# q and k of the third late unit loaded into the free tile of x, and the visits of the first late segment set anew

## The chip, the core and the metric

The kernel runs on one core of one Trainium2 chip. The metric is the device time of an execution in microseconds (us). The kernel before took 726.04 us (median of 3 runs, 725.66 to 726.95). The profiled execution is one of them, the one of 725.66 us; the span from its first to its last instruction is 723.9 us.

## What is computed

Attention over chunks, then one gated feed-forward layer. q, k and v are [4, 8, 768, 64] (batch, heads, sequence, head size); every chunk of 32 queries sees 8 memory positions, 16 positions to the left, its own 32 and 8 to the right. The result is laid out as 3072 tokens of 512 values and goes through the second part.

```python
for c in range(nc):                                   # 24 chunks of 32 queries
    k_full = np.concatenate([mem_k, k[:, :, l_start:r_end]], axis=2)
    v_full = np.concatenate([mem_v, v[:, :, l_start:r_end]], axis=2)
    a = softmax(scale * np.matmul(q_c, k_full.transpose(0, 1, 3, 2)))
    out[:, :, c_start:c_end] = np.matmul(a, v_full)
...
xn = x / rms * rms_g                                  # x: 3072 x 512
g = xn @ w_gate                                       # 512 x 1536
silu = g * (1.0 / (1.0 + np.exp(-g)))
return (silu * (xn @ w_val) @ w_out)                  # w_out: 1536 x 512
```

## The kernel before

**Units, blocks, segments.** Attention is cut into 32 units: one unit is one batch, one half of its sequence (384 queries, 12 chunks) and two heads. Four units fill one block, 384 tokens by 512 values, held in a tile `x`. There are 8 blocks. The feed-forward part goes block by block: for each of 12 columns f of the hidden layer TensorE (PE) makes g (12 matmuls of 128x384, `pg`, L591) and v (12 more, `pv`, L591), and one column later the output part (9 matmuls of 128x512, `po`, L629). Each f32 matrix is split in a high and a low part, so every product takes three matmuls. Between them the other engines make the hidden value of the column: ACT `t` (tanh, L598), DVE `t` (L602, which reads `pg` and frees it; L605, which reads `pv`), ACT `hh` (its high part, a cast, L255), DVE `hl` (its low part, L614). The output part reads `hh` in its first two matmuls of three and `hl` in the third. `t`, `hh`, `hl`, `pg` and `pv` have one buffer each.

**The written-out part.** Units 0 to 15 and their feed-forward columns are in a string of tokens, `ORDER`, that sets every engine's order by hand. It covers blocks 0 and 1: columns 0 to 4 of block 0 and all 12 of block 1 (items 0 to 16 of `SEQ`; item 15 is column 10 of block 1, item 16 its column 11). Near its end stand the tokens R0 to R4 for the first late unit, unit 16 (batch 2, first half, heads 0 and 1): R0 loads its q and k, R2 transposes them, R4 loads its v. The string ends with `o14 I Ha R3 L v16 k15a l15 h16 o15 i16 j16`: the matmuls v of item 16, the cast `hh` of item 15 on ACT (k15a), its `hl` on DVE (l15), its output part on PE (o15).

**The late part.** After it come the segments: columns 5 to 11 of block 0 (the first late segment), then blocks 2 to 7. PE's order there is that of the code; a scheduler places the other engines' instructions by priority. Units 16 to 31 are made in pairs by `late_steps`, in steps that the table `VISITS` puts into gaps of a segment: gap 2(f - first f) stands behind the g of column f, the next gap behind its v. Step "v" of pair n holds the PE work: the transposes `pT` (L377) of the pair before, the scores `s` (L346) of pair n, the outputs `o` (L398) of the pair before; then DVE writes the outputs into `x` (`stage_r`). It also transposes q and k of the first unit of pair n + 1 on DVE (`stage_t`, behind the last DVE instruction placed so far). Step "t" does so for the second unit of that pair and loads the first one of pair n + 2. Step "n" scales a finished block. A block's `x` is turned (`xT`, L470) and split at the end of its segment.

**A late unit's loads.** `load_qk` issues 8 DMAs on SP's queue, 4 of q (L193) and 4 of k (L195), by turns. They fill the tiles `qn` and `kn`, one buffer each, so a unit's loads wait until DVE has transposed the unit before (L315 twice for q, L320 once for k). `load_v` first has ACT copy the memory's values into the unit's v tile (`kv<-memV`, L255), POOL adds ones (L214), and SP issues 5 DMAs of v (L228, L239). For unit 16 the tile `memV` is filled anew for batch 2 by two DMAs on SP's queue (L210) ahead of that copy. After its transposes two small copies on ACT (L328, L329) finish a unit's k. DMAs of one queue are issued in order, and an instruction that waits holds all behind it on its engine.

The late tiles of one unit of a pair share buffers with tiles of the first part: `late_buffers(0)` clears a tile (`qp`, L132) just after the written-out part.

Of the kernel before, what the change touches and what calls it, by code (L numbers as in the profile page):

```python
# [8 lines left out]
F32 = mybir.dt.float32  # L9
# [10 lines left out]
CH = 32  # L20
LC, RC = 16, 8
KC = NM + LC + CH + RC
DM, FF = 512, 1536
P = 128
NG = H // 2
HT = 384
NT = HT // P
NC = HT // CH
# [6 lines left out]
YMAX = 0x1DFE / 0x1000 * 2.0 ** -96  # L35


VISITS = (((1, "v"), (4, "t"), (5, "v"), (8, "t"), (11, "v"), (12, "n")),
# [31 lines left out]
def tile_kernel(ctx: ExitStack, tc: tile.TileContext, q, k, v, mem_k, mem_v,  # L70
# [3 lines left out]
    p1 = ctx.enter_context(tc.tile_pool(name="p1", bufs=1))  # L74
# [33 lines left out]
    def on_pe(ins):  # L108
        if pinned:
            tc.keep_in_program_order(ins)  # L110

    def psum_a(name):
        return psa.tile([P, 512], F32, name=name, tag="at")

    def psum_m(tag, name):
        return psm.tile([P, 512], F32, name=name, tag=tag)


    NE = NG * 2
# [42 lines left out]
    def pt_of(u):  # L162

        return pts[1 + u % 2] if u < NE else late["pt", 1 - u % 2]
# [9 lines left out]
    def load_qk(u):  # L174
        b, hf, g = units[u]
        h0 = 2 * g
        t0 = hf * HT
        d = st.setdefault(u, {})
        if u < NE:

            k0 = t0 - hf * CH
            for n, src, r0, rows in (("q", q, t0, HT), ("k", k, k0, HT + CH)):
                x = d[n] = early.tile([P, 8, D], F32, name=f"{n}f{u}", tag=f"{n}f{u % NG}")[0:rows // 4]
                nc.sync.dma_start(out=x.rearrange("p (h r) d -> p h (r d)", h=2),
                                  in_=src[b, h0:h0 + 2, r0:r0 + rows].rearrange("h (p r) d -> p h (r d)", r=4))
            return

        d["q"] = qn = p1.tile([P, NC, CH], F32, name=f"qn{u}", tag="qn")
        d["k"] = kn = p1.tile([P, NC + 1, CH], F32, name=f"kn{u}", tag="kn")
        k0 = t0 - hf * CH  # L190
        for w in range(4):
            hh, e = w // 2, CH * (w % 2)
            nc.sync.dma_start(out=qn[CH * w:CH * w + CH],  # L193
                              in_=q[b, h0 + hh, t0:t0 + HT, e:e + CH].rearrange("(c p) d -> p c d", p=CH))
            nc.sync.dma_start(out=kn[CH * w:CH * w + CH],  # L195
                              in_=k[b, h0 + hh, k0:k0 + HT + CH, e:e + CH].rearrange("(c p) d -> p c d", p=CH))

    def load_v(u):
        stage_v(u)
        dma_v(u)  # L200

    def stage_v(u, e="a"):
        b, hf, g = units[u]
        h0, h1 = 2 * g, 2 * g + 2
        t0 = hf * HT
        d = st.setdefault(u, {})
        d["v"] = vw = unit_tile(u, [P, NJ, 2, D + 1], "vw", NG)
        if hf == 0 and g == 0 and b > 0:
            for cp in range(2):
                nc.sync.dma_start(out=memV[64 * cp:64 * cp + NM], in_=mem_v[b].rearrange("h m d -> m h d"))  # L210

        mv = memV[:, h0:h1].unsqueeze(1).broadcast_to([P, NJ, 2, D])
        copy(e, vw[:, :, :, 0:D], mv)
        nc.gpsimd.tensor_copy(out=vw[:, :, :, D], in_=ones[hf])  # L214

    def dma_v(u, e="s"):
        b, hf, g = units[u]
        h0, h1 = 2 * g, 2 * g + 2
        t0 = hf * HT
        vw = st[u]["v"]  # L220
        W = KC - NM
        for cp in range(2):
            base = 64 * cp
            s0 = t0 + CH * cp - LC
            ja, jb = 0, NJ
            eng = nc.scalar if e == "a" else nc.sync
            if hf == 0 and cp == 0:
                eng.dma_start(out=vw[base + NM + LC:base + KC, 0, :, 0:D],  # L228
                              in_=v[b, h0:h1, 0:W - LC].rearrange("h s d -> s h d"))
                ja = 1  # L230
            if hf == 1 and cp == 1:
                r0 = s0 + 64 * (NJ - 1)
                eng.dma_start(out=vw[base + NM:base + KC - RC, NJ - 1, :, 0:D],
                              in_=v[b, h0:h1, r0:r0 + W - RC].rearrange("h s d -> s h d"))
                jb = NJ - 1
            for hh in range(2):
                vs = v[b, h0 + hh]
                src = bass.AP(vs.tensor, vs.offset + (s0 + 64 * ja) * D, [[D, W], [64 * D, jb - ja], [1, D]])
                eng.dma_start(out=vw[base + NM:base + KC, ja:jb, hh, 0:D], in_=src)  # L239
# [64 lines left out]
    def stage_t(u):  # L304

        stage_ta(u)
        new_kw(u)
        stage_tb(u)
        stage_tc(u)
# [40 lines left out]
    def stage_m(u):  # L350
        stage_ma(u)
        stage_mb(u)
# [18 lines left out]
    def stage_p(u, tag=None):  # L371
        d = st[u]
        tag = tag or (None if u >= NG else "o0")
        t = psum_m(tag, f"pT{u}") if tag else psum_a(f"pT{u}")
        pe = d["p"].rearrange("p j k -> p (j k)")
        for i in range(NT):
            on_pe(nc.tensor.transpose(out=t[:, i * P:(i + 1) * P], in_=pe[:, i * P:(i + 1) * P], identity=ident))  # L377
        d["t"] = t
# [10 lines left out]
    def stage_o(u, tag=None):  # L389
        d = st[u]  # L390
        pt = pt_of(u)
        tag = tag or (None if u >= NG else f"o{1 + u % 2}")
        o = psum_m(tag, f"o{u}") if tag else psum_a(f"o{u}")
        for i in range(NT):
            for hh in range(2):
                for par in range(2):
                    c0 = (2 * i + hh) * (D + 1)
                    on_pe(nc.tensor.matmul(o[64 * par:64 * par + 64, c0:c0 + D + 1],  # L398
                                     lhsT=pt[:, i, 2 * par + hh].rearrange("p c q -> p (c q)"),
                                     rhs=d["v"][:, 2 * i + par, hh, :], start=True, stop=True))  # L400
        d["o"] = o
# [313 lines left out]
    def new_x():  # L715
        return p1.tile([P, NT, H, D], F32, name="x", tag="x")
# [3 lines left out]
    def behind_last(u):  # L720
        done = next(i for i in reversed(nc.cur_bb.bb.instructions) if i.engine == nc.vector.engine)
        with tc.issue_after(done):
            stage_t(u)

    def late_steps():


        pairs = [(u, u + 1) for u in range(NE, len(units), 2)]
        for n in range(len(pairs) + 1):
            old = pairs[n - 1] if n else ()  # L730
            cur = pairs[n] if n < len(pairs) else ()
            new = pairs[n + 1] if n + 1 < len(pairs) else ()
            for u in old[0:1]:
                if u % NG == 0:
                    late_x["x"] = new_x()
            x = late_x.get("x")
            with tc.high_priority():
                for i, u in enumerate(old):
                    stage_p(u, None if i else "g")
                for u in old:  # L740
                    stage_c(u)
            if not cur:
                yield "p"
            with tc.high_priority():
                for u in cur:
                    stage_s(u)
                for u in cur:
                    stage_m(u)
                for u in cur:
                    stage_e(u)  # L750
                for i, u in enumerate(old):
                    stage_o(u, "v" if cur and i else None)
                for u in old:
                    stage_r(u, x)
                for u in new[0:1]:
                    behind_last(u)
            for u in new[0:1]:
                load_qk(u + 1)
            for u in cur if n else ():
                load_v(u)  # L760
            yield "v"
            if n and n % 2 == 0:
                with tc.high_priority():
                    stage_n(x)
                yield "n"
            if new:
                with tc.high_priority():
                    behind_last(new[1])
                if n + 2 < len(pairs):
                    load_qk(pairs[n + 2][0])  # L770
            yield "t"

    x = new_x()
# [28 lines left out]
    def tok_R(n):  # L802
        if n == 0:
            load_qk(NE)
        if n == 1:
            late_buffers(1)
        if n == 2:
            stage_t(NE)
        if n == 3:
            late_pt()  # L810
        if n == 4:
            load_v(NE)
            load_qk(NE + 1)

    def tok_N(n):
        sp["ss"] = stage_n0(blk["x"])
# [83 lines left out]
        late_buffers(0)  # L900
        stage_t(NE + 1)
    load_v(NE + 1)
    load_qk(NE + 2)
    pinned.append(True)

    def split_x(x, first, rest):
# [17 lines left out]
    for sg, (blk, f0) in enumerate(segments):  # L924
        po = [psm_o(i) for i in range(NT)] if sg else sp["po", 0]
        last = sg == len(segments) - 1
        steps = {} if last else dict(VISITS[min(sg, 2) + (sg == len(segments) - 2)])

# [57 lines left out]
```

## Time and profile before

| | before |
|---|---|
| median of 3 runs | 726.04 us |
| the profiled execution | 725.66 us |
| its span | 723.9 us |
| granted TensorE clock, mean | 0.995 |
| busy: PE, DVE, ACT, POOL | 708.6, 382.1, 284.2, 35.5 us |
| mean DMA rate | 69 GB/s |

Times in the profile count from the span's start. A row of the timeline gives start, duration, engine, line, operation, out<-in, shape, count, and in brackets the idle time of the engine before it with what ended it. A row of the waits gives who waited for whom, the sum, the count and the longest. A row of the stages gives start:end, its length, then each engine's busy time with its count, the granted TensorE clock (1.00 is full speed), the share of the DMA engines and GB/s.

### The profile page before, as it was taken

To read this page: it belongs to the slowest core of one execution; us is meant where nothing else is said; L and a number is where in the kernel's file an instruction comes from. 1 tells how busy PE (TensorE), PEld (TensorE's weight loads), DVE (VectorE), ACT (ScalarE), POOL (GpSimd) and SP (SyncE) were. 2 spreads that over 40 slices of the span, in tenths; PEclk is the share of its full clock that TensorE was granted. 3 is DMA by queue.
4 is the path that set the end of the run, shared out by engine and by line. 5 is a ranking of instruction groups with operands and counts; after the bars stand their busy time and mean duration, and the time that the engine had idled before them with its cause. 6 is when DMAs were issued, how large, how long until landed. Compare 5 with 4: busy or idle time off the path is not lost.

```text
span 723.9 us, 13126 instructions
## 1 busy us (share of the span) xinstructions
PE 708.6 (98%) x5136; PEld 656.0 (91%) x5136; DVE 382.1 (53%) x727; ACT 284.2 (39%) x600; POOL 35.5 (5%) x143
## 2 busy tenths in 40 slices
PE   7889999999999999999999999999999999999997
PEld 7778999998989999999999999999998999999997
DVE  3888999975663625444273534536254332432222
ACT  4899666543353315332153312433143221331112
POOL 3300000010010001000010000000010000000000
PEclk8999999999999999999999999999999999999999
DMA  8994554425532402304041120413111110010001
GB/s 173 206 255 147 175 194 127 125 46 123 97 60 75 78 9 42 77 11 84 0 77 52 34 53 1 84 44 66 18 35 28 44 39 1 1 45 0 1 1 43
DMA packets 143173, 50.20 MB, mean 69 GB/s; under 512 B 126984, under 2 KB 134536, under 8 KB 143112
## 3 DMA queue, kind: packets, MB, share of 16 engines
q1 hardware_dynamic: 139832, 44.49, 26.8%
q10 hardware_dynamic: 3280, 4.88, 1.9%
q8 instruction: 40, 0.66, 0.4%
q14 instruction: 21, 0.17, 0.1%
HBM read 43.06 MB, written 6.29 MB: 68 GB/s over the span
## 4 chain that ended last, share of the span: by engine, by line
PE 89%; ACT 4%; DVE 2%; DMA 2%; issue 1%; SPq 1%; POOL 0%; ACTq 0%; DVEq 0%; POOLq 0%
PE po L629 27%; PE pv L591 26%; PE pg L591 26%; PE s L346 3%; PE o L398 2%; PE xT L470 1%; PE pT L377 1%; ACT junk L428 1%; DMA memV<-in_mem_v_dram 1%; ACT pt L255 1%; DMA kv<-in_v_dram 1%; ACT qb L255 0%; ACT wy L539 0%; ACT ws L538 0%; SPq L195 0%
## 5 line engine op out<-in xcount | busy, mean ns | idle before, releaser
L591 PE MATMUL pg<-xh,wh_g 128*128 128x384 f32 x384 | 130.0, 339 | 0.7 <-DVE t L602 0.7
L591 PE MATMUL pv<-xh,wl_v 128*128 128x384 f32 x384 | 129.5, 337 | 0.5 <-DVE wl_v L562 0.5
L591 PE MATMUL pv<-xh,wh_v 128*128 128x384 f32 x384 | 129.7, 338 | 0.0
L591 PE MATMUL pv<-xl,wh_v 128*128 128x384 f32 x384 | 129.6, 337 | 0.0
L591 PE MATMUL pg<-xh,wl_g 128*128 128x384 f32 x384 | 129.5, 337 | 0.0
L591 PE MATMUL pg<-xl,wh_g 128*128 128x384 f32 x384 | 129.4, 337 | 0.0
L255 ACT CAST hh<-t 128x384 fp32r<-128x384 f32 x95 | 48.6, 512 | 201.9 <-PE po L629 177.8
L629 PE MATMUL po<-wh_o,hh 128*128 128x512 f32 x285 | 114.7, 402 | 0.3
L629 PE MATMUL po<-wh_o,hl 128*128 128x512 f32 x285 | 113.1, 397 | 0.0
L602 DVE SCALAR_TENSOR_TENSOR t<-t,pg 128x384 f32<-128x384 f32 x96 | 53.0, 552 | 112.8 <-ACT t L598 112.4
L629 PE MATMUL po<-wl_o,hh 128*128 128x512 f32 x285 | 112.3, 394 | 0.0
L614 DVE TENSOR_TENSOR hl<-t,hh 128x384 fp32r<-128x384 f32 x95 | 52.5, 553 | 104.7 <-ACT hh L255 99.9
L598 ACT ACTIVATE t<-pg 128x384 f32<-128x384 f32 x96 | 47.1, 491 | 122.8 <-PE pg L591 114.9
L605 DVE TENSOR_TENSOR t<-t,pv 128x384 f32<-128x384 f32 x95 | 52.5, 553 | 75.5 <-PE pv L591 74.9
L591 PEld LDWEIGHTS pg<-xh,wh_g 128*128 128x128 f32 x384 | 72.0, 188 | 4.6 <-DVE t L602 0.9
L591 PEld LDWEIGHTS pg<-xl,wh_g 128*128 128x128 f32 x384 | 72.1, 188 | 3.5
L591 PEld LDWEIGHTS pv<-xh,wl_v 128*128 128x128 f32 x384 | 72.0, 188 | 0.8 <-DVE wl_v L562 0.8
L591 PEld LDWEIGHTS pv<-xh,wh_v 128*128 128x128 f32 x384 | 72.1, 188 | 0.4
L591 PEld LDWEIGHTS pv<-xl,wh_v 128*128 128x128 f32 x384 | 72.1, 188 | 0.3
L591 PEld LDWEIGHTS pg<-xh,wl_g 128*128 128x128 f32 x384 | 72.0, 188 | 0.0
L629 PEld LDWEIGHTS po<-wh_o,hl 128*128 128x128 f32 x285 | 53.5, 188 | 14.4 <-DVE hl L614 2.0
L629 PEld LDWEIGHTS po<-wh_o,hh 128*128 128x128 f32 x285 | 53.5, 188 | 10.5 <-ACT hh L255 1.7
(124 smaller groups left out, 772.3 us busy)
## 6 DMA issues: line engine op xcount, KB each, us to landing
kn<-in_k_dram SPq DMA_DIRECT2D x96, 52.0 KB
qn<-in_q_dram SPq DMA_DIRECT2D x96, 48.0 KB
out_dram<-ob ACTq DMA_DIRECT2D x18, 256.0 KB
ws<-in_moe_w_gate_dram SPq DMA_DIRECT2D x4, 1024.0 KB
ws<-in_moe_w_val_dram SPq DMA_DIRECT2D x4, 1024.0 KB
ws<-in_moe_w_out_dram SPq DMA_DIRECT2D x4, 1024.0 KB
kv<-in_v_dram SPq DMA_DIRECT2D x48, 84.0 KB
kv<-in_v_dram SPq DMA_DIRECT2D x48, 70.0 KB
```

The costliest lines, as they stand in the source:

```text
L255: return nc.scalar.copy(out, in_)
L346: on_pe(nc.tensor.matmul(s[64 * par:64 * par + 64, o:o + KC], lhsT=qb[:, c].rearrange("p s q -> p (s q)"), rhs=kw[:, c], start=True, stop= ...
L377: on_pe(nc.tensor.transpose(out=t[:, i * P:(i + 1) * P], in_=pe[:, i * P:(i + 1) * P], identity=ident))
L398: on_pe(nc.tensor.matmul(o[64 * par:64 * par + 64, c0:c0 + D + 1], lhsT=pt[:, i, 2 * par + hh].rearrange("p c q -> p (c q)"), rhs=d["v"][: ...
L428: nc.scalar.activation(junk[:, 0:(g1 - g0) * P], x[:, i, 2 * g0:2 * g1].rearrange("p h d -> p (h d)"), AF.Square, accum_out=ss[:, i:i + 1])
L470: on_pe(nc.tensor.transpose(out=t[:, i * P:(i + 1) * P], in_=tiles[i][:, kt * P:(kt + 1) * P], identity=ident))
L591: on_pe(nc.tensor.matmul(ps[:, 0:HT], lhsT=weight(a, n, f, kt), rhs=xs[c][:, kt], start=cnt == 0, stop=cnt == 3 * NKT - 1))
L598: nc.scalar.activation(t, g, AF.Tanh, scale=0.5)
L602: nc.vector.scalar_tensor_tensor(out=t, in0=t, scalar=1.0, in1=g, op0=ALU.add, op1=ALU.mult)
L605: nc.vector.tensor_tensor(out=t, in0=t, in1=vv, op=ALU.mult)
L614: nc.vector.tensor_tensor(out=hl, in0=t, in1=hh.bitcast(F32), op=ALU.subtract)
L629: on_pe(nc.tensor.matmul(po[i], lhsT=h[a][:, i * P:(i + 1) * P], rhs=weight(c, "o", f), start=f == 0 and n == 0, stop=f == NF - 1 and n == 2))
```

## The change

- **A tile of its own for q and k of unit 18, the third late unit (L188, L189).** Until step "v" of the second pair, nothing is in the tile of `x`, since blocks 0 and 1 are done with it. Unit 18 loads q and k into one tile `qkn` with the tag "x". So its loads no longer wait for unit 17's transposes, and unit 19 takes the turn of 18 in `qn` and `kn`.
- **Loads one turn earlier (L811 to L813, L903, L757, L769).** Token R4 now loads q and k of unit 17 first, then v of 16, then q and k of 18. Behind the written-out part stand v of 17 and q and k of 19 (before: 18). Step "v" of the first pair loads nothing more.
- **The first transposes of the third pair (L753 to L756).** In the second pair's step "v", `stage_t` of unit 20 now stands ahead of `stage_r` of units 16 and 17, and not behind it.
- **Visits of the first late segment (L38).** The first "t" moves from gap 4 to 2, the third "v" from 11 to 9, and "n" from 12 to 10. The other segments keep theirs.

What is computed is the same, and so is the number of each engine's instructions but for rows of SP that are counted apart.

```diff
-VISITS = (((1, "v"), (4, "t"), (5, "v"), (8, "t"), (11, "v"), (12, "n")),
+VISITS = (((1, "v"), (2, "t"), (5, "v"), (8, "t"), (9, "v"), (10, "n")),
...
-        d["q"] = qn = p1.tile([P, NC, CH], F32, name=f"qn{u}", tag="qn")
-        d["k"] = kn = p1.tile([P, NC + 1, CH], F32, name=f"kn{u}", tag="kn")
+        if u == NE + 2:
+
+            t = p1.tile([P, NT * DM], F32, name=f"qkn{u}", tag="x")
+            d["q"] = qn = t[:, 0:NC * CH].rearrange("p (c d) -> p c d", d=CH)
+            d["k"] = kn = t[:, NC * CH:(2 * NC + 1) * CH].rearrange("p (c d) -> p c d", d=CH)
+        else:
+            d["q"] = qn = p1.tile([P, NC, CH], F32, name=f"qn{u}", tag="qn")
+            d["k"] = kn = p1.tile([P, NC + 1, CH], F32, name=f"kn{u}", tag="kn")
...
+                for u in new[0:1] if n == 1 else ():
+                    behind_last(u)
                 for u in old:
                     stage_r(u, x)
-                for u in new[0:1]:
+                for u in new[0:1] if n != 1 else ():
                     behind_last(u)
-            for u in new[0:1]:
+            for u in new[0:1] if n else ():
                 load_qk(u + 1)
...
         if n == 4:
+            load_qk(NE + 1)
             load_v(NE)
-            load_qk(NE + 1)
+            load_qk(NE + 2)
...
     load_v(NE + 1)
-    load_qk(NE + 2)
+    load_qk(NE + 3)
```

Three places of the engines' orders follow, before and now (now the code's lines stand 6 to 10 lower; the number behind a tile's name tells one buffer's use from the next).

SP's queue from the end of unit 16's q and k (`qn_1844`, `kn_1845`) on; `kv_1882` is unit 16's v tile. Before:

```order
L195 DMA kn_1845<-in_k_dram 32x13x32 [waits DMAHW4_49]
L210 DMA memV<-in_mem_v_dram 8x8x64 [waits DMAHW5_49]
L210 DMA memV<-in_mem_v_dram 8x8x64 [waits DMAHW6_49]
L228 DMA kv_1882<-in_v_dram 40x2x64 [waits DMAHW7_49,DVE_49,Pool_49]
L239 DMA kv_1882<-in_v_dram 56x5x64 [waits DMAHW0_49]
```

Now, with `qn_1910` and `kn_1911` for unit 17:

```order
L201 DMA kn_1845<-in_k_dram 32x13x32 [waits DMAHW4_49]
L199 DMA qn_1910<-in_q_dram 32x12x32 [waits DMAHW5_49,DMAHW3_49,DMAHW7_49,DMAHW1_49,DVE_49]
L201 DMA kn_1911<-in_k_dram 32x13x32 [waits DMAHW4_49,DMAHW2_49,DMAHW6_49,DMAHW0_49,DVE_49]
L199 DMA qn_1910<-in_q_dram 32x12x32
L201 DMA kn_1911<-in_k_dram 32x13x32
L199 DMA qn_1910<-in_q_dram 32x12x32
L201 DMA kn_1911<-in_k_dram 32x13x32
L199 DMA qn_1910<-in_q_dram 32x12x32
L201 DMA kn_1911<-in_k_dram 32x13x32
L216 DMA memV<-in_mem_v_dram 8x8x64 [waits DMAHW5_49]
L216 DMA memV<-in_mem_v_dram 8x8x64 [waits DMAHW6_49]
L234 DMA kv_1882<-in_v_dram 40x2x64 [waits DMAHW7_49,Pool_49]
```

The two DMAs of `memV` stood right behind unit 16's loads; now unit 17's eight stand between, and the first two of these wait for DVE.

DVE behind the written-out part, from item 16's `t` (L605) on. Before:

```order
L605 TENSOR_TENSOR t<-t,pv 128x384 [waits DVE_49,PE_49]
L132 MEMSET qp_1976 128x1536
L614 TENSOR_TENSOR hl<-t,hh 128x384 [waits PE_49,Activation_49]
L315 STREAM_TRANSPOSE qp_1976<-qn_1919 64x12x32 [waits DMAHW6_49,DMAHW4_49,DVE_49]
L602 SCALAR_TENSOR_TENSOR t<-t,pg 128x384 [waits Activation_49]
L315 STREAM_TRANSPOSE qp_1976<-qn_1919 64x12x32 [waits DMAHW2_49,DMAHW0_49]
L320 STREAM_TRANSPOSE kv_1978<-kn_1920 128x13x32 [waits DMAHW5_49,DMAHW7_49,DMAHW3_49,DMAHW1_49]
```

Now:

```order
L611 TENSOR_TENSOR t<-t,pv 128x384 [waits DVE_49,PE_49]
L132 MEMSET qp_1985 128x1536
L326 STREAM_TRANSPOSE kv_1987<-kn_1911 128x13x32 [waits DMAHW4_49,DMAHW6_49,DMAHW2_49,DMAHW0_49]
L321 STREAM_TRANSPOSE qp_1985<-qn_1910 64x12x32 [waits DMAHW7_49,DMAHW5_49,DVE_49]
L321 STREAM_TRANSPOSE qp_1985<-qn_1910 64x12x32 [waits DMAHW3_49,DMAHW1_49]
L620 TENSOR_TENSOR hl<-t,hh 128x384 [waits PE_49,Activation_49]
L608 SCALAR_TENSOR_TENSOR t<-t,pg 128x384 [waits Activation_49]
```

Unit 17's three transposes moved ahead of item 16's `hl`.

DVE in the first late segment, from the `hl` of column 6 to the reader of column 7's `pg`. Before:

```order
L614 TENSOR_TENSOR hl<-t,hh 128x384 [waits PE_49,Activation_49]
L315 STREAM_TRANSPOSE qp_1976<-qn_2095 64x12x32 [waits DMAHW5_49,DMAHW4_49]
L315 STREAM_TRANSPOSE qp_1976<-qn_2095 64x12x32 [waits DMAHW6_49,DMAHW2_49]
L320 STREAM_TRANSPOSE kv_1978<-kn_2096 128x13x32 [waits DMAHW3_49,DMAHW7_49,DMAHW1_49,DMAHW0_49]
L602 SCALAR_TENSOR_TENSOR t<-t,pg 128x384 [waits Activation_49]
```

Now, from unit 18's and 19's transposes on:

```order
L326 STREAM_TRANSPOSE kv_1882<-qkn_1929 128x13x32 [waits DMAHW7_49,DMAHW5_49,DMAHW1_49]
L321 STREAM_TRANSPOSE qp_1985<-qn_2003 64x12x32 [waits DMAHW2_49,DMAHW0_49]
L326 STREAM_TRANSPOSE kv_1987<-kn_2004 128x13x32 [waits DMAHW5_49,DMAHW7_49,DMAHW3_49,DMAHW1_49]
L608 SCALAR_TENSOR_TENSOR t<-t,pg 128x384 [waits Activation_49]
L611 TENSOR_TENSOR t<-t,pv 128x384 [waits DVE_49,PE_49]
L620 TENSOR_TENSOR hl<-t,hh 128x384 [waits PE_49,Activation_49]
L608 SCALAR_TENSOR_TENSOR t<-t,pg 128x384 [waits Activation_49]
```

Unit 19's transposes moved from between column 6's `hl` and column 7's reader (L602, now L608) to ahead of column 6's reader.

## The prediction

> **What bounds the kernel now.** I read the page first, then PE's waits, then the timeline of each engine around them.
>
> ```profile
> span 723.9 us, 13126 instructions
> PE 708.6 (98%) x5136; PEld 656.0 (91%) x5136; DVE 382.1 (53%) x727; ACT 284.2 (39%) x600; POOL 35.5 (5%) x143
> ```
>
> PE works nearly all the time. So only PE's gaps can be won, and any new gap costs its whole length. PE's waits from 100 us on, with the sum, the count and the longest:
>
> ```profile
> PE pT L377 <- DVE t L602: 1.4, 1, 1.4
> PE xT L470 <- DVE x L451: 0.4, 1, 0.4
> ...
> 220.00:700.00 480.00, 479.79 (x3310) 446.95 (x3310) 204.46 (x409) 143.88 (x330) 14.26 (x59) 1.00 0.17 37
> ```
>
> There are two, both in the first late segment; the stage row from 220 to 700 shows PE at 479.79 of 480. The change can win 1.4 + 0.4 = 1.8 us and no more. The first gap in the timeline:
>
> ```profile
> 177.22 0.49 ACT L598 ACTIVATE t<-pg 128x384 f32<-128x384 f32 x1 [1.84 <-PE pg L591]
> 177.41 0.47 SPq L195 DMA_DIRECT2D kn<-in_k_dram  x1
> 178.87 0.58 DVE L315 STREAM_TRANSPOSE qp<-qn 64x384 f32<-64x384 f32 x1 [1.25 <-DMA qn<-in_q_dram]
> 179.63 0.61 DVE L320 STREAM_TRANSPOSE kv<-kn 128x416 f32<-128x416 f32 x1 [0.18 <-DMA kn<-in_k_dram]
> 180.17 0.52 DVE L602 SCALAR_TENSOR_TENSOR t<-t,pg 128x384 f32<-128x384 f32 x1
> 180.74 0.55 PE L377 MATMUL pT<-ident,kv 128*128 128x128 f32 x3 [1.44 <-DVE t L602]
> ```
>
> Column 7's `pg` could be read from 177.71, when ACT ends, but DVE stands before unit 19's transposes until its DMAs land. PE needs that buffer for `pT`.
>
> **What is won.** Unit 18 has its own tile, so unit 19's loads wait for unit 17's transposes alone, and unit 19's own now stand ahead of column 6's reader. Then nothing of DMA is between column 7's g and its reader: the 1.4 goes. The third "v" and "n" come two gaps earlier, so `x` is scaled a whole column before `xT` needs it: the 0.4 goes too. The PE work of the moved visits is the same, since the same matmuls stand between a v and a `po` one column earlier. Sum: minus 1.8, if nothing else becomes late there (below).
>
> **What the queue of SP costs.** Two engines around the end of the written-out part, first SP and DVE, then ACT and PE:
>
> ```profile
> 145.86 0.73 SPq L210 DMA_DIRECT2D memV<-in_mem_v_dram  x2
> 153.31 1.17 DVE L315 STREAM_TRANSPOSE qb<-qn 64x384 f32<-64x384 f32 x2
> 154.52 0.61 DVE L320 STREAM_TRANSPOSE kv<-kn 128x416 f32<-128x416 f32 x1
> ...
> 155.58 0.84 ACT L255 COPY kv<-memV 128x768 f32<-128x768 f32 x1
> 156.80 0.63 ACT L255 CAST wh_o<-wy 128x512 fp32r<-128x512 f32 x1 [0.38 <-DVE wy L554]
> 157.33 0.51 ACT L255 CAST hh<-t 128x384 fp32r<-128x384 f32 x1
> 157.61 0.63 DVE L562 TENSOR_TENSOR wl_o<-wy,wh_o 128x512 fp32r<-128x512 f32 x1
> 158.15 0.55 DVE L614 TENSOR_TENSOR hl<-t,hh 128x384 fp32r<-128x384 f32 x1
> 158.34 0.40 PE L629 MATMUL po<-wh_o,hh 128*128 128x512 f32 x1
> 158.81 0.45 PE L629 MATMUL po<-wh_o,hl 128*128 128x512 f32 x1
> ```
>
> `memV` was asked for at 145.86, ten us before ACT's copy. Now its two DMAs queue behind unit 17's eight, and these wait for unit 16's transposes, the last of which ends at 154.52 + 0.61 = 155.13. How long eight take behind a transpose is seen at a later unit:
>
> ```profile
> 188.00 0.61 DVE L320 STREAM_TRANSPOSE kv<-kn 128x416 f32<-128x416 f32 x1
> 188.64 0.32 SPq L195 DMA_DIRECT2D kn<-in_k_dram  x1
> ...
> 191.56 0.47 SPq L195 DMA_DIRECT2D kn<-in_k_dram  x1
> ```
>
> The last of the eight is out at 192.03, 3.4 us behind the transpose's end. So `memV` is issued at 158.6 and, its second half, at 159.0. From issue to the reader: 1.97 to 2.22 us for q and k above (177.41 to 179.63). For `memV` itself the DMA view, in slices of 0.1 us from 145 on, bounds it from below:
>
> ```profile
> DMA  9983399721699413995333311100000000000000
> ```
>
> The last packets end at 147.6, 1.3 us behind the second issue (146.3). So ACT can copy between 160.3 and 161.2; I take 160.8, since a semaphore follows the last packet. ACT works in order, and behind the copy stand the cast of `wh_o` and item 15's `hh`. From 160.8: copy 0.84, `wh_o` 0.63, overlapped to 0.53 (156.80 to 157.33), `hh` 0.51, done at 162.7. DVE behind it: `wl_o` from 162.2, `hl` from 162.8 to 163.35. PE's third matmul of item 15 started 0.11 behind `hl` (158.70 to 158.81), so now at 163.46 instead of 158.81. PE has nothing else to do, as its order is fixed: **plus 4.65**, from 4.15 to 5.05 by the two landing times.
>
> **What the moved transposes cost.** Item 16's `hl` and the matmuls around it:
>
> ```profile
> 160.74 1.34 DVE L132 MEMSET qp<- 128x1536 f32 x1 [0.27 <-PE po L629]
> 162.00 0.49 DVE L614 TENSOR_TENSOR hl<-t,hh 128x384 fp32r<-128x384 f32 x1
> 162.61 0.39 PE L629 MATMUL po<-wh_o,hh 128*128 128x512 f32 x1
> 163.07 0.39 PE L629 MATMUL po<-wh_o,hl 128*128 128x512 f32 x1
> ```
>
> Unit 17's three transposes now come between the memset and `hl`: 1.17 + 0.61 = 1.78. Their data are there by then (issued until 158.6). `hl` ended at 162.49, on this clock now at 164.27, and the third matmul follows at 164.38 instead of 163.07: **plus 1.3**. Both chains hang on item 15's `hl`, so the first delay does not hide the second. Without one: 0, if PE comes later to item 16 for another reason.
>
> **What I cost at nothing.** Unit 19's loads: from ACT's copy on SP issues 5 + 8 + 5 + 8 pieces at some 0.5 us, so the last lands near 177.3 and column 6's reader runs by 178.5. PE then needs that `pg` for column 7 near 174.8 + 5.9 = 180.7 (column 7's g ended at 177.2 and takes some 2.4); without this cover, what is late shows in full. Unit 20's transposes, now ahead of units 16's and 17's writes of `x`: the last write, and column 8's v, which needs the buffer of unit 17's output:
>
> ```profile
> 186.32 0.56 DVE L421 TENSOR_TENSOR x<-o,r 128x384 f32<-128x384 f32 x1
> ...
> 189.02 2.12 PE pv L591 x12
> ```
>
> 189.02 - 186.88 = 2.14 against 1.78 leaves 0.36; if that is gone, some 0.3 is paid. Two gaps less for the third pair are covered by loads that now run ahead of it.
>
> Sum without any change of the clock: 725.66 - 1.8 + 4.65 + 1.3 = 729.8.
>
> **The clock.** A PE idle for four microseconds has a row in this trace, near the start, and one window at the end that was half idle:
>
> ```profile
> 8.45:11.87 3.42, 0.94 (x26) 0.76 (x25) 0.46 (x2) 3.35 (x8) 2.78 (x14) 1.00 1.09 208
> 11.87:15.28 3.41, 3.41 (x27) 3.11 (x22) 1.46 (x3) 0.82 (x4) 0.62 (x3) 0.50 1.07 197
> 15.28:18.69 3.41, 3.41 (x35) 2.99 (x34) 1.40 (x4) 2.53 (x6) 0.39 (x2) 0.50 0.68 160
> 18.69:22.10 3.41, 3.23 (x49) 2.62 (x49) 2.66 (x6) 2.64 (x7) 0.39 (x2) 1.00 1.13 212
> 718.42:721.84 3.42, 1.68 (x8) 1.03 (x6) 0.42 (x1) 1.58 (x3) 0.00 (x0) 1.00 0.48 175
> ```
>
> Behind a window of 3.42 us with 0.94 busy (28%) the granted clock was 0.50 for 6.8 us; with 1.68 busy (49%) it stayed. The new gap idles PE for 4.3 us, so some window of 3.41 is at most 37% busy, and in most positions under 28%. I expect 0.50 for 3.4 to 6.8 us, one or two such windows. Up to 2.2 us of them still lie in the gap; the other 1.2 to 6.6 are busy and lose half, 0.6 to 3.3. Item 16's wait of 1.3 is then hidden in part or whole, since DVE keeps its pace while PE, slowed, comes later to the matmul that needs `hl`. Net 0 to plus 2 over the sum; I take 1.0, as most positions of the windows give the longer loss but two windows were seen only where PE's work was small matmuls: **730.8**.
>
> The Trainium skill's page "TensorE: Matmul & The Clock Gate" (section "Part 1: The HAM clock gate") says that the half rate comes only after a whole idle window of some 3.4 us, in windows that run free of the kernel. By that rule 4.3 us hold a whole window in some 26% of the positions only, and the time would mostly be 729.8. The trace differs: its window before the half rate was 28% busy.
>
> **The rivals.**
> - *Clock stays.* Both waits, 729.8. For it: the early window's work was small matmuls, which may count for less. Against it: the rows above. 0.28.
> - *`memV` in time, the second wait alone.* 725.66 - 1.8 + 1.3 = 725.2, the same within 0.2%. It needs `memV` landed by 156.1 (155.58 and the 0.5 between the end of `hh`, 157.84, and its use at 158.34), so unit 17's loads would have to leave 4 us before DVE is done; the order's waits speak against it. 0.07.
> - *Faster.* No new wait: also the transposes end before `hl` is needed. 725.66 - 1.8 = 723.9, the other side. It decides at the same 156.1, and at 0.3 us for `hl`. 0.08.
> - *More than forecast.* 6.8 us at half clock with nothing hidden, or a late unit 19: 729.8 + 3.3 = 733.1 and above. 0.06.
>
> **How the numbers follow.** The forecast, both waits and a halved clock, has 0.51. The profiled execution lies 0.4 under the median of the runs shown, which reach 1.3 above it; I leave 730.8 and let the range hold that. It goes from 728.4 (clock stays, `memV` early by 0.5, the second wait half hidden) to 733.0. 0.2% is 1.45 us, about what a measurement of this kernel can tell from no change. Faster 0.08, same 0.07, slower 0.85.
>
> **What would show it.** `memV` issued near 158.6; ACT's copy of it waiting for a DMA until near 160.8; PE idle some 4.3 us before a `po` near 158.5; granted clock 0.50 behind it; item 16's `hl` behind three transposes; no wait of `pT` for `t` near 185, none of `xT` for `x`. The forecast is wrong if the copy of `memV` starts near 155.6, or if PE shows no gap above 1 us behind 150.

## The result and the profile after

The changed kernel takes 730.92 us (median of 5 runs, 729.7 to 731.49), the kernel before beside it 726.95 us (725.66 to 727.11): a ratio of 1.0051, 95% interval 1.0037 to 1.0065. It is slower by 4.0 us, and the interval reaches from 2.7 to 4.7 us. The profiled execution of the changed kernel took 731.13 us, its granted clock is 0.991 in the mean.

The head of its page:

```profile
span 729.4 us, 13123 instructions
PE 711.4 (98%) x5136; PEld 658.7 (90%) x5136; DVE 382.1 (52%) x727; ACT 284.2 (39%) x600; POOL 36.1 (5%) x143
```

PE has the same 5136 matmuls and 2.8 us more of busy time (711.4 against 708.6), with the span 5.5 us longer: so some of the loss is a gap, and some is matmuls that took longer. PE's waits from 100 us on:

```profile
PE po L635 <- ACT hh L261: 4.1, 1, 4.1
```

The waits of `pT` and of `xT` are gone, and one of 4.1 us has come. The chain of waits in order of time (start, us, what) tells from where:

```profile
155.31 0.62 DVE kv L326
...
156.31 0.47 SPq L199
...
159.39 0.37 SPq L216
...
159.81 1.71 DMA memV<-in_mem_v_dram
...
161.60 0.83 ACT kv L261
162.44 0.52 ACT wh_o L261
162.96 0.42 ACT hh L261
...
163.42 4.21 PE po L635 x9
167.63 2.98 PE pg L597 x12
170.60 2.07 PE po L635 x9
172.68 2.12 PE pv L597 x12
...
187.14 0.66 PE pT L383 x6
```

Read from the top: unit 16's last transpose on DVE, unit 17's loads on SP, `memV`'s two DMAs, their landing, ACT's copy, the casts of `wh_o` and of item 15's `hh`, PE. In the kernel before, item 15's `po` followed on PE's own v without a wait; now the chain reaches it through DVE, SP, a DMA and ACT. The two rows behind are as telling: the `po` of item 15 took 4.21 us and the `pg` behind it 2.98, where the next `po` and `pv`, with as many matmuls, took 2.07 and 2.12. The stages of that stretch, with the granted clock third from the right:

```profile
159.18:162.59 3.41, 0.12 (x1) 0.00 (x0) 0.00 (x0) 0.99 (x2) 0.09 (x1) 1.00 0.29 48
162.59:166.01 3.42, 2.59 (x6) 2.00 (x7) 2.29 (x4) 1.99 (x4) 1.77 (x7) 0.50 0.45 103
166.01:169.42 3.41, 3.41 (x11) 3.02 (x11) 3.15 (x5) 1.02 (x3) 0.00 (x0) 0.50 0.50 81
169.42:172.83 3.41, 3.41 (x18) 3.03 (x17) 0.79 (x2) 1.81 (x4) 0.00 (x0) 1.00 0.62 124
```

The rows are cut where the granted clock changes. The gap fills one window of 3.41 us but for 0.12 us and reaches 0.83 us into the next, and two windows at 0.50 follow. The busy column reads 3.41 at half clock as at full clock; only the count tells (11 matmuls started in it, against 18 in the next).

### The profile page after: what moved, and what is told of

It is laid out like the page before. It is cut to its first block, busy times and chain, and to the rows that moved or that the text cites. A ratio compares the mean times of both kernels' runs of the same rounds, so it can differ in the third digit from the quotient of the medians.

```text
span 729.4 us, 13123 instructions
## 1 busy us (share of the span) xinstructions
PE 711.4 (98%) x5136; PEld 658.7 (90%) x5136; DVE 382.1 (52%) x727; ACT 284.2 (39%) x600; POOL 36.1 (5%) x143
## 4 chain that ended last, share of the span: by engine, by line
PE 91%; ACT 3%; DMA 2%; DVE 2%; issue 1%; SPq 0%; POOL 0%; ACTq 0%; DVEq 0%; POOLq 0%
PE po L635 28%; PE pv L597 27%; PE pg L597 27%; PE s L352 3%; PE o L404 2%; PE pT L383 1%; PE xT L476 1%; DMA ws<-in_moe_w_val_dram 1%; DMA memV<-in_mem_v_dram 1%; ACT junk L434 0%; ACT qb L261 0%; ACT ws L544 0%; ACT pt L261 0%; ACT wy L545 0%; DVE kw L264 0%
## 5 line engine op out<-in xcount | busy, mean ns | idle before, releaser
L608 DVE SCALAR_TENSOR_TENSOR t<-t,pg 128x384 f32<-128x384 f32 x96 | 53.1, 553 | 116.3 <-ACT t L604 116.0
```

The source lines that it names most:

```text
L608: nc.vector.scalar_tensor_tensor(out=t, in0=t, scalar=1.0, in1=g, op0=ALU.add, op1=ALU.mult)
```

## Theories

- **T (the forecast).** The loss is SP's queue: `memV` stands behind unit 17's eight loads, and the copy of it holds `hh`. The half clock behind the gap adds a part. `pT` and `xT` are won as planned.
- **R1.** The loss comes from what else was moved: the x tile, the visits, the transposes ahead of item 16's `hl`.
- **R2.** The half clock, not the wait itself, is the larger part of it.

## Experiments

**1. `memV` first, all else as changed.** `stage_v` issues `memV`'s DMAs and ACT's copy.

```diff
         if n == 4:
+            stage_v(NE)
             load_qk(NE + 1)
-            load_v(NE)
+            dma_v(NE)
             load_qk(NE + 2)
```

> The change with one order mended: token R4 asks for memV first (stage_v of unit 16), then loads q and k of unit 17, then v of 16 and q and k of 18. Theory (memV's two DMAs stand behind unit 17's eight on SP, which wait for DVE): ACT's copy of memV starts near 156 again, PE's gap before item 15's output part (4.3 us) goes, the clock stays at 1.00 there. Only one of unit 17's three transposes now stands ahead of item 16's hl, for a wait of 0 to 0.2. The gains stay: pT's wait 1.4 to 1.6, xT's 0.4 to 0.9. Time 2.2 under the kernel before: 724.7, ratio 0.997. Rival (the loss comes from the crowded loads, the moved transposes or the tile in x): still 729 to 731, ratio 1.003 to 1.006.

Measured: 724.93 us (7 runs, 723.89 to 726.39) against 727.28 for the kernel before, which ran anew beside experiments 1 to 4 (24 runs) and 5 to 7 (23 runs, 727.13); ratio 0.9960, 95% interval [0.9945, 0.9975]. Rows of the timeline of SP, ACT and DVE:

```profile
147.41 0.72 SPq L216 DMA_DIRECT2D memV<-in_mem_v_dram  x2
157.17 0.84 ACT L261 COPY kv<-memV 128x768 f32<-128x768 f32 x1
163.59 0.55 DVE L326 STREAM_TRANSPOSE kv<-kn 128x416 f32<-128x416 f32 x1
164.06 0.51 DVE L620 TENSOR_TENSOR hl<-t,hh 128x384 fp32r<-128x384 f32 x1
```

The copy has no bracket: it waits for no DMA. Its chain of waits, from the `po` of item 15 on:

```profile
160.10 2.13 PE po L635 x9
162.22 2.11 PE pg L597 x12
164.34 2.18 PE po L635 x9
...
180.99 0.66 PE pT L383 x6
```

PE runs through, with no wait from 100 us on and no half clock there. Issuing these two DMAs first has turned a loss of 4.0 us into a gain of 2.35 us (1.8 to 4.0). The x tile, the visits and the earlier loads are all still in, so they don't make the loss. The scheduler put only one transpose of unit 17 ahead of item 16's `hl` here, so this run does not test that part of R1; experiment 7 does.

**2. The same, and item 16's `hl` ahead of all three transposes by hand.**

```diff
-g16 j15 J L R2 R4 f F o14 I Ha R3 L v16 k15a l15 h16 o15 i16 j16
+g16 j15 J L R2 R4 f F o14 I Ha R3 L v16 k15a l15 h16 o15 i16 j16 k16a l16
...
-    with tc.high_priority():
-        prev = moe_hl(sp["t", last1], moe_hh(sp["t", last1]))
+    prev = sp["h", len(SEQ) - 1]
```

> The kernel of the run with memV first, and item 16's hh and hl written out by hand at the end of the order string, so that hl stands ahead of the memset and of unit 17's transposes on DVE. Theory: little is left to win there at full clock with one transpose ahead, 0 to 0.2 under the run with memV first: 724.6, ratio 0.997. Rival (the wait for hl is the larger part of the loss): 1 us or more under it.

Measured: 725.07 us (9 runs), ratio 0.9964 [0.9951, 0.9977]: the same as the first. One transpose (0.55 us) ahead of `hl` costs nothing that can be measured.

**3. The kernel before with only the third pair's visits moved.**

```diff
-VISITS = (((1, "v"), (4, "t"), (5, "v"), (8, "t"), (11, "v"), (12, "n")),
+VISITS = (((1, "v"), (4, "t"), (5, "v"), (8, "t"), (9, "v"), (10, "n")),
```

> The kernel before with one part of the change: in the first late segment the third v goes from gap 11 to 9 and n from 12 to 10; all loads as before. Theory: xT's waits for x go (0.4 to 0.9), pT's wait of 1.4 at 180 stays: 726.2, ratio 0.999. Rival (the earlier visits crowd the first late segment and bring waits of their own): 727 or more, ratio 1.000 or above, with a wait of pT or o near 200.

Measured: 726.20 us (12 runs) against 727.28, ratio 0.9979 [0.9966, 0.9992], a gain of 0.6 to 2.5 us. PE's waits:

```profile
PE pT L377 <- DVE t L602: 1.6, 1, 1.6
```

And its chain of waits, at `pT` and at `xT`:

```profile
182.89 0.87 PE pT L377 x6
...
216.14 0.98 PE xT L470 x9
```

`xT`'s wait is gone and `pT`'s stays, so each belongs to its own part of the change. The gain is above the 0.4 of the wait row; the chain of the kernel before says why:

```profile
180.74 0.87 PE pT L377 x6
...
214.37 1.38 PE xT L470 x9
...
218.20 0.50 PE po L629
```

Its nine `xT` took 1.38 us and here 0.98. `x` was being scaled in three pieces, two on DVE and one on ACT, which ended at 214.31, 214.55 and 214.71; the first three transposes started at 214.37, 214.60 and 214.77, some 0.06 behind each, and from the fourth on one every 0.11. These are gaps too short for the table of waits. So the wait was worth 0.4 + 0.4. For `pT` likewise 0.87 behind a wait and 0.66 without one (experiment 1): 1.44 + 0.2.

**4. The gap filled.** The changed kernel with v of item 16 made three times in place (the same 12 matmuls, the sum begun anew each time), so that PE is busy while `memV` comes.

```diff
...
+        for turn in range(1 + again):
+            cnt = 0
...
-        sp["v", n] = moe_in("v", SEQ[n][1], xs01[SEQ[n][0]])
+        sp["v", n] = moe_in("v", SEQ[n][1], xs01[SEQ[n][0]], again=2 if n == 16 else 0)
```

> The changed kernel with PE kept at work in the gap: the 12 matmuls of v of item 16 are made three times over, 4.2 us of added matmuls that give the same sums, just ahead of the output part of item 15 that waits for memV. Theory (the half clock behind the gap costs some 2.4 and hides the 1.3 of item 16's hl): the granted clock stays at 1.00 from 150 to 180, the output part starts when it did, the wait for item 16's hl shows as 1.2 to 1.4, and the time is 1.1 under the changed kernel: 729.8, ratio 1.004. Rival (the clock plays no part in the time): the added matmuls just fill the gap and the time stays at 731, or the added work costs and it is above.

Measured: 730.41 us (9 runs) against 727.28, ratio 1.0039 [1.0026, 1.0053]; the interval overlaps the changed kernel's, so the times do not separate the clock's part. The profile does. Its stages, at the same bounds:

```profile
159.18:162.59 3.41, 3.41 (x22) 3.41 (x21) 0.00 (x0) 0.23 (x1) 0.00 (x0) 1.00 0.42 70
162.59:166.01 3.42, 2.43 (x10) 1.51 (x10) 1.71 (x3) 2.58 (x5) 1.86 (x7) 1.00 0.25 58
166.01:169.42 3.41, 3.41 (x19) 3.01 (x18) 3.03 (x6) 1.29 (x5) 0.00 (x0) 1.00 0.66 119
```

With PE busy in the gap the clock stays at 1.00, so the idle PE is what the half clock followed. From the `po` of item 15 to the v of column 5 it took 6.81 us (164.18 to 170.99), the changed kernel 9.09 (163.42 to 172.51), the kernel before 6.33. So the slowed stretch cost 2.3 to 2.8 us, more than item 16's term of 1.3. Why the time did not drop by as much is seen in the timeline of SP and PE:

```profile
157.08 1.53 SPq L199 DMA_DIRECT2D qn<-in_q_dram  x1
...
160.19 0.72 SPq L216 DMA_DIRECT2D memV<-in_mem_v_dram  x2
...
164.18 0.50 PE L636 MATMUL po<-wh_o,hh 128*128 128x512 f32 x1 [0.91 <-ACT hh L261]
```

One issue of a load took 1.53 us instead of 0.47, so `memV` was out at 160.19, 5.14 us behind the first of unit 17's loads, where the changed kernel took 4.08 (155.31 to 159.39). PE waited 0.91 us even behind its filling, so the filling itself held nothing up. This run keeps the wait (5.3 us from v to `po` beyond the kernel before: 7.41 against 2.11) without the half clock, and is still slower than before by its whole interval. In the changed kernel's own profile the wait is 4.28 us (157.03 to 163.42, less 2.11) and the slowed stretch 2.76 (9.09 less 6.33). So the half clock is the smaller part, and R2 falls. Only one transpose stood ahead of item 16's `hl` here, so its wait didn't show, though it was expected to.

**5. The kernel before with only R4's two lines swapped.**

```diff
         if n == 4:
+            load_qk(NE + 1)
             load_v(NE)
-            load_qk(NE + 1)
```

> The kernel before with one line moved: token R4 loads q and k of unit 17 ahead of v of unit 16; no tile in x, old visits. Theory (this order alone makes the loss): memV is asked for near 159, PE idles 4 to 4.5 us before item 15's output part, the clock is halved behind it in most runs (2 to 2.5), pT's wait of 1.4 to 1.6 goes since PE comes later to it, xT's 0.8 stays. Time some 5 over the kernel before: 732, ratio 1.004 to 1.008. Rival (it takes the tile in x or the visits to make the loss): within 1 us of the kernel before, ratio 0.999 to 1.001.

Measured: 732.02 us (6 runs) against 727.13, ratio 1.0070 [1.0051, 1.0088]. Two swapped lines lose 3.7 to 6.4 us, as much as the whole change or more. PE's waits:

```profile
PE po L629 <- ACT hh L255: 4.1, 1, 4.1
PE xT L470 <- DVE x L451: 0.4, 1, 0.4
```

And its stages, cut where its clock changes:

```profile
161.09:164.50 3.41, 0.34 (x2) 0.30 (x2) 0.78 (x2) 1.76 (x3) 1.26 (x6) 1.00 0.09 18
164.50:167.91 3.41, 3.41 (x9) 2.38 (x8) 2.48 (x4) 1.21 (x2) 0.59 (x2) 0.50 0.55 124
167.91:171.30 3.39, 3.39 (x18) 3.11 (x18) 2.71 (x6) 1.77 (x5) 0.00 (x0) 1.00 0.60 119
```

The same gap of 4.1 us and a half clock behind it, of one window here. `xT`'s wait is still there, as no visit was moved. `pT`'s is gone although neither the x tile nor the visits are in. That can be the earlier turn of unit 17's loads or PE's coming some 6 us later; experiment 6, where PE is not late, tells them apart.

**6. Experiment 1 without the x tile.** Unit 18 loads into `qn` and `kn` like any other.

```diff
-        if u == NE + 2:
+        if False:
```

> The kernel with memV first, but unit 18 loads into qn and kn again, so it waits for unit 17's transposes, and unit 19 for unit 18's. Theory (the tile in x takes the wait of pT away): pT waits again for column 7's reader, which stands behind unit 19's transposes; since the loads still run ahead of v by one turn, the wait is 0.3 to 1.4, time 725.3 to 726.4, ratio 0.9975 to 0.999. Rival (the earlier turn of the loads alone does it, the tile adds nothing): no wait of pT, 725, ratio 0.996 as with the tile.

Measured: 725.12 us (12 runs) against 727.13, ratio 0.9971 [0.9957, 0.9986]; with the x tile it was 0.9960 [0.9945, 0.9975], not to be told apart. DVE before column 7's reader, in the timeline:

```profile
181.49 0.61 DVE L326 STREAM_TRANSPOSE kv<-kn 128x416 f32<-128x416 f32 x1
182.02 0.52 DVE L608 SCALAR_TENSOR_TENSOR t<-t,pg 128x384 f32<-128x384 f32 x1
```

PE behind it, in the chain of waits:

```profile
180.46 2.12 PE pv L597 x12
...
182.60 0.87 PE pT L383 x6
```

The reader still stands behind unit 19's transposes and ends at 182.54, PE is free at 182.58: 0.02 us of waiting and 0.2 of a slower first `pT` (0.87 against 0.66). So the earlier turn of the loads wins most of `pT`'s wait, as the rival had it. The tile adds some 0.2 us in the profile and nothing that the times can tell; 0.3 to 1.4 had been expected of it.

**7. Three transposes ahead of item 16's `hl`, at full clock.** Experiment 1, with the order of the changed kernel set by hand (R5: `late_buffers(0)`, R6: `stage_t` of unit 17).

```diff
-g16 j15 J L R2 R4 f F o14 I Ha R3 L v16 k15a l15 h16 o15 i16 j16
+g16 j15 J L R2 R4 f F o14 I Ha R3 L v16 k15a l15 h16 o15 i16 j16 R5 k16a R6 l16
```

> The kernel with memV first, and by hand all three transposes of unit 17 between the memset and item 16's hl on DVE, with its hh ahead of unit 17's copies on ACT: the changed kernel's order of DVE, but at full clock and without the gap before item 15. Theory (the second wait of the forecast, hidden by the half clock in the changed kernel's profile): PE waits 1.2 to 1.4 before the third matmul of item 16's output part, time 1.3 over the run with hl ahead: 726.4, ratio 0.998. Rival (DVE is early enough, the second wait was never there): no such wait, 725, ratio 0.996.

Measured: 725.61 us (12 runs) against 727.13, ratio 0.9977 [0.9961, 0.9994]. PE's one wait from 100 us on, in the timeline at item 16:

```profile
164.81 0.50 PE L635 MATMUL po<-wh_o,hl 128*128 128x512 f32 x1 [1.21 <-DVE hl L620]
```

At full clock the three transposes do hold item 16's third matmul, by 1.2 us. The time shows less than that: it is 0.5 us above experiment 2's, not 1.3, and the two intervals overlap, so the size rests on the profile alone. With the three transposes ahead of `hl` and `memV` first the kernel is still not slower than before. So that order doesn't make the loss either, and R1 falls as a whole.

## Why the prediction was right, step by step

The forecast was 730.8 and the median is 730.92; slower, as forecast. That it fits to 0.1 us is luck in the base: the sum started from 725.66, the fastest of the runs of before, so it forecast plus 5.1. The medians differ by 4.0, and the interval of that difference ends at 4.7. The two profiles differ by 5.5, of which 0.8 is older than the change: v of item 16, ahead of any new wait, starts at 156.23 before and at 157.03 after (one row of each kernel's timeline):

```profile
156.23 0.34 PE L591 MATMUL pv<-xh,wh_v 128*128 128x384 f32 x1
...
157.03 0.34 PE L597 MATMUL pv<-xh,wh_v 128*128 128x384 f32 x1
```

The steps are held against the traces without this 0.8. The rows of the changed kernel's timeline that the steps need, PE's and then DVE's:

```profile
164.44 0.63 PE L635 MATMUL po<-wh_o,hl 128*128 128x512 f32 x1
170.91 0.39 PE L635 MATMUL po<-wh_o,hl 128*128 128x512 f32 x1
172.51 0.34 PE L597 MATMUL pv<-xh,wh_v 128*128 128x384 f32 x1
186.98 0.49 PE L383 MATMUL pT<-ident,kv 128*128 128x128 f32 x3
223.58 0.50 PE L635 MATMUL po<-wh_o,hh 128*128 128x512 f32 x1
...
167.46 0.55 DVE L326 STREAM_TRANSPOSE kv<-kn 128x416 f32<-128x416 f32 x1
167.94 1.13 DVE L321 STREAM_TRANSPOSE qp<-qn 64x384 f32<-64x384 f32 x2
169.10 0.56 DVE L620 TENSOR_TENSOR hl<-t,hh 128x384 fp32r<-128x384 f32 x1
```

| step | forecast | measured |
|---|---|---|
| `memV` issued | 158.6 | 159.39 - 0.80 = 158.59 |
| ACT's copy of it starts | 160.8 | 161.60 - 0.80 = 160.80 |
| item 15's third matmul later by | 4.65 | 164.44 - 158.81 - 0.80 = 4.83 |
| from there to item 16's third matmul (item 16's `hl` 1.3, clock 1.0 net) | 2.3 | 170.91 - 163.07 - 5.63 = 2.21 |
| `pT`'s wait gone | -1.4 | 186.98 - 180.74 - 7.84 = -1.60 |
| `xT`'s wait gone | -0.4 | 223.58 - 218.20 - 6.24 = -0.86 |
| sum | 5.15 | 4.58 |

- **SP's queue** was right in mechanism and size, to 0.2 us. Item 15's `hl` ended at 164.17 - 0.80 = 163.37, where the forecast had 163.35; what is left is PE's slower clock. Experiment 1 takes it away alone and experiment 5 brings it in alone.
- **Item 16's `hl` and the clock** are right as a sum and wrong in their parts. The slowed stretch cost about all of the 2.2 to 2.75 us (the last from PE's first matmul of item 15), and the wait for `hl` nothing: `hl` ends at 169.66, PE, slowed, comes to its first matmul only at 170.44. The forecast had it hidden "in part or whole", and whole is what happened in the profiled execution. In experiment 7's profile, where the clock stays, the wait is 1.2, close to the 1.3.
- **What is won** was under-sized, and "no more" than 1.8 was wrong. It was read from the waits alone and is 2.46: a restart behind a wait and a piecewise wait are no rows there (experiment 3).
- **What was costed at nothing** held. Unit 19's loads had less cover than the 2.2 forecast: column 6's reader ended at 182.03, and PE's g of column 7 came at 182.90, 0.87 later. It was not the loads that came late: DVE had no idle time from 176.20 to 182.03, with unit 18's and unit 19's transposes ahead of the reader. Unit 20's transposes ahead of `x` cost no gap.
- **The rival "clock stays"** has one run that may belong to it, that of 729.7 us. Its mean clock is 0.997, which leaves room for about one slow window of 3.41 us (half a window in 728 us is 0.0023). The profiled run, at 0.991, has four, two of them near the start. No trace shows where the window of that run lay. The Trainium skill's page "TensorE: Matmul & The Clock Gate" (section "Part 1: The HAM clock gate") has the half rate follow an idle window of some 3.4 us. The traces differ: the window ahead of the half clock had 0.12 us busy of 3.41 in the changed kernel, 0.34 in experiment 5 and up to 1.60 elsewhere (last section). Wherever a gap of 4.1 us lies, it leaves one window with at most 1.4 us busy (3.41 - 4.1 / 2). So by these traces, and as an estimate, the half clock follows such a gap in every position, and the 0.28 for "clock stays" looks too large. No run set the gap across two windows on purpose.

The loss of the two swapped lines alone is 4.9 us between the medians, 0.9 above that of the whole change. It is not further above because experiment 5 wins most of `pT`'s wait too: 1.5 us from v of column 5 to the scores behind `pT` (16.87 us before, 15.34 there). Of the 2.46 it lacks mainly `xT`'s 0.86. Its profiled execution lost less at the gap, 5.99 us against 7.04 from v of item 16 to v of column 5 (8.44 us before), as it had one slow window and not two.

## What to carry to other kernels

A load that is moved up in a queue pushes back what stood there: look for what has a nearer due time, and follow its reader's engine to the work queued behind that reader. Here two small DMAs, issued late, made PE's work 4.8 us later, and 7.0 with the slowed stretch behind, and a version that keeps their place has the whole gain of the change (724.93 against 727.28 us). Size what a vanished wait is worth from the chain, start to start, and not from the table of waits; and where a new gap on PE is as long as the 4.1 us here, expect the work behind it to be slow as well, which may in turn hide the next wait.

## What the runs showed of the hardware

- **What brings the half clock.** In all nine traces the clock changes on a grid of 3.41 us, and the half clock lasts 3.41, 6.83 or 10.24 us unless the end cuts it off. Cut on that grid, each of the 16 full-rate windows with at most 1.60 us of PE busy time was followed by one at half rate (the largest: 1.60, experiment 1 from 46.86; 1.58, experiment 3 from 7.30; 1.22, experiment 4 from 9.58). None with 1.67 us or more was (the smallest: 1.67, experiment 1 from 9.32 and the kernel before from 718.43; 1.72, experiment 2 from 717.78). So here the line lies near half a window of work, not at an idle window.
- **How long it lasts.** Behind nearly the same gap (4.1 us) it lasted two windows in the changed kernel and one in experiment 5. In the first PE was busy in 2.59 of 3.42 us of the first slow window, in the second in all of it. A wholly busy window doesn't end it everywhere: near the start, one slow window with 3.41 us busy was enough in experiment 2 (from 11.22), and in the kernel before (from 11.87) a second one followed. What decides this is not shown.
- **What it costs.** In the changed kernel a matmul of 128x512 started 0.43 us behind the one ahead of it at half clock and 0.23 at full clock, one of 128x384 0.32 and 0.18: a factor of 1.8 to 1.9, not 2.
- **What a DMA issue takes.** A single issue on SP's queue took 0.28 to 0.6 us in nearly all rows between 140 and 260 us, most often 0.47. In each of the nine traces one to three of them took 1.1 to 1.8 us, with no cause that the profile shows. The one in experiment 4 (1.53) stood ahead of `memV` and put it out 1.1 us later.
